# More dense filler products in a recurrent-attention and gated-MLP kernel, a longer warm-up, and two last stores on another queue

## The chip, the cores and the metric

The kernel runs on one core of a Trainium2 chip. The metric is the device time of one execution in microseconds (us), from the launch to the last store. TensorE (PE in the rows) multiplies matrices into PSUM, VectorE (DVE), ScalarE (ACT) and GpSimd (POOL) work element by element, and SyncE (SP) issues nearly all transfers. Each engine runs its instructions in program order. TensorE's clock has two levels here, 1.2 and 2.4 GHz; the rows give it as the granted clock, 0.50 or 1.00.

## What is computed

All inputs are float32. Three stages follow each other:

```python
for t in range(S):                                    # B, H, S, D = 4, 8, 768, 48
    cur = einsum('bhd,bhe->bhde', u * k[t], v[t])
    y[t] = einsum('bhd,bhde->bhe', r[t], state + cur)
    state = w * state + einsum('bhd,bhe->bhde', k[t], v[t])
x = y as [B * S, 384]
x = ((x @ w_a) * (x @ w_b)) @ w_out                   # 384 -> 1536 -> 384
out = (((x @ w1) * (x @ w2)) @ w3) @ w_out2           # 384 -> 1024 -> 1024 -> 384
```

## The kernel before

**The recurrence in chunks.** The 768 steps are cut into six chunks of 128 tokens (a chunk is called a step below, 0 to 5), each for four batches: 24 units, unit u being batch u % 4 of step u // 4. A unit computes scores r k with decay tables already multiplied in (`scores_h`, lines 365 and 369), the diagonal term with `u` (`scores_d`, line 377, whose moving operand has two columns), masks them on VectorE (`h_mask`, line 389), puts the diagonal in (`h_diag`, line 392), copies the rest on ScalarE (lines 397 and 400), and multiplies by the values: `y_0` (lines 499 and 504) for the units of step 0, which have no state yet, `y_mm` (lines 479 and 484) for step 1, with the state. The result is split into a high and a low part (lines 511, 514 and 517 in step 0; 537, 541 and 546 in step 1), because each large product is done as three: high by high, high by low and low by high.

**The large products.** `ab_mm` (line 639) multiplies the outputs by `w_a` and `w_b`, `m_mm` (lines 656 to 658) by `w_out`; both are mixed with the units of later steps. The weights arrive as 64-bit floats (`raw`, issued at lines 942 and 944) and are turned into float32 by three VectorE operations (lines 974, 978 and 982) and split into high and low (ScalarE line 987, VectorE line 990). The second pair of layers follows the same pattern with a table of sums (line 1293) and ends with `o` (lines 1396 to 1398), four evictions (lines 1417 and 1419) and the stores (line 1424).

**Filler products.** `busy(ps, n)` at line 284 multiplies the identity matrix by n copies of itself and writes 128 * n columns that nothing reads. It is called at three places: for the warm-up at the start (line 293, the table `WARM` of line 40), and at the end of `scores_d` for the units of step 0 (line 380), in the upper columns of the same PSUM bank as the diagonal, so that `h_diag` waits for it as well. A product of plain float32 operands is two records in the trace.

**The order.** `plan` (line 97) is a list scheduler: tasks with an engine, a cost estimate, dependencies, buffers and a priority are placed greedily, and each engine's program order is the order in which they were placed. The numbers given to `task` (0.9 at line 814, 0.4 at line 877, 5.8 at line 788) are such estimates; other numbers can give another order everywhere behind them.

Of the kernel before, what the change touches and what calls it, by code (L numbers as in the profile page):

```python
# [18 lines left out]
B, H, S, D = 4, 8, 768, 48  # L19
NP = H // 2  # L20
C = 128
# [3 lines left out]
KD = DM // 128  # L25
# [11 lines left out]
N64 = 61  # L37
SQ_LO, SQ_HI = 2e-9, 1e10

WARM = (4, 4, 4, 2)  # L40

SPLIT = 6
PAD = 288
# [125 lines left out]
def rwkv_moe_kernel(ctx, tc, rkT, nat, wu, wab, wout, w12, w3T, wo2, r_in, k_in, v_in, w_in, u_in, out):  # L169
# [13 lines left out]
    with tc.manual_schedule():  # L183
# [11 lines left out]
        def at_tile(shape):  # L195
            return psp.tile(shape, F32, tag=at_next[0], name=at_next.pop(0)[:-1])
# [87 lines left out]
        def busy(ps, n):  # L284

            mm(ps.rearrange("p (n c) -> p n c", n=n), lhsT=ident,
               rhs=ident.rearrange("p (o c) -> p o c", o=1).to_broadcast([128, n, 128]), start=True, stop=True)
# [83 lines left out]
        def scores_d(u):  # L371

            ps = at_tile([128, 512])
            at_ps["d", u] = ps[:, 0:H]
            e = alt[u % B][0:112, 2]
            for p in range(NP):
                mm(at_ps["d", u].rearrange("p (x n) -> p x n", x=2)[:, :, p], lhsT=e[:, p * C:(p + 1) * C], rhs=u_x[:, p],
                   start=(p == 0), stop=True, skip_group_check=True)
            if u < B:
                busy(ps[:, 256:512], 2)  # L380

        def bc4(t):
            return t.rearrange("p (o n) -> p o n", o=1).to_broadcast([128, 4, HALF])
# [104 lines left out]
        def y_0(u):  # L488

            vz = vz_t[u % 2]  # L490
            ps = at_ps["y", u] = at_tile([128, KD, C])
            a = a_t.pop(u)

            for n, e in enumerate((HALF, 128)):
                cs = slice(n * HALF, (n + 1) * HALF)
                for k in range(KD):
                    for x in range(2):
                        c = out_at(2 * k + x)
                        mm(ps[c:c + 64, k, cs], lhsT=vz[0:e, k, x, :], rhs=a[0:e, n, 4 * x + 3, :],  # L499
                           start=(k == 0 and n == 0), stop=False, skip_group_check=True)  # L500
                    for x in range(2):
                        h = 2 * k + x
                        c = out_at(h)
                        mm(ps[c:c + D, k, cs], lhsT=v_0[0:e, u, h * D:(h + 1) * D], rhs=a[0:e, n, 4 * x + k, :],
                           start=False, stop=True, skip_group_check=True)
# [164 lines left out]
        def task(*a, **k):  # L670
            t = Task(*a, **k)
            for b in t.bufs:
                b.users.append(t)
            tasks.append(t)
            return t

        def use(t, *bufs):
            for b in bufs:
                b.users.append(t)
            return t  # L680
# [93 lines left out]
        def due(us):  # L774
            return -3000.0 + 10 * us
# [9 lines left out]
            return [use(task("ACT", 0.6, lambda u=u: h_low(u), [ev], pu), ba)] + of  # L785

        tab = task("DVE", 5.2, lambda: None, [], due(-9))
        task("PE", 5.8, lambda: None, [], due(-9))
        task("ACT", 2.4, lambda: None, [], due(-9))
        task("POOL", 1.8, lambda: None, [], due(-9))  # L790
        m_one = [Slot(f"m{k}") for k in range(KD)]
# [9 lines left out]
        for u in range(B):  # L801
            pu = due(5 + 4 * u)
            rk_b[u] = fixed(W[("w1h", "w1l", "w2h", "w2l")[u]])
            W[("w4h", "w4l", "w5h", "w5l")[u]].users = alt_b[u].users
            lr = task("SP", 0.45, lambda u=u: load_rk(u), [], due(u), [rk_b[u]], size=0.45)
            lv = load_v[u] = task("SP", 0.45, lambda u=u: load_nat(u), [], due(u), [v_b] if u == 0 else [], size=0.19)
            use(lv, v_b)
            pz = use(task("ACT", 0.25, lambda u=u: prep_0(u, 3), [lv] + y_last.get(u - 2, []), pu), vz_b[u % 2], v_b)
            pu_ = use(task("POOL", 1.3, lambda u=u: prep_0(u, 2), [lr], pu), rk_b[u], alt_b[u])
            pk = use(task("DVE", 0.7, lambda u=u: prep_0(u, 0), [lr, tab], pu, sbuf=True), rk_b[u], alt_b[u])  # L810
            pr = use(task("DVE", 0.7, lambda u=u: prep_0(u, 1), [lr, tab, pk], pu, sbuf=True), rk_b[u], alt_b[u])
            bt, bd = [Buf(banks + at_s, none) for _ in range(2)], Buf(m_one, none)
            sc = use(task("PE", 1.2, lambda u=u, bt=bt: picked(bt, lambda: scores_h(u)), [pk, pr], pu, bt), alt_b[u])
            sd = use(task("PE", 0.9, lambda u=u, bd=bd: picked([bd], lambda: scores_d(u)), [sc, pu_], pu, [bd]), alt_b[u])
            m_old.append(sd)
            ba = Buf(a0_s, none)
            ev = halves(u, pu, sc, sd, bt, bd, ba)
            m_old += ev
            by = Buf(at_s, none)
            y = use(task("PE", 2.2, lambda u=u, by=by: picked([by], lambda: y_0(u)), ev + [pz], pu + 1, [by]),  # L820
                    ba, v_b, vz_b[u % 2])
            y_last[u] = [y]
            yh = use(task("ACT", 0.5, lambda u=u: y_0_evac(u), [y], pu + 2, [x_b[0]] if u == 0 else []), by, x_b[0])
            yr = use(task("PE", 0.2, lambda u=u: y_0_rest(u), [yh], pu + 2), by, x_b[0])
            xl_0.append(use(task("ACT", 0.5, lambda u=u: y_0_low(u), [yr], pu + 2), by, x_b[0]))
# [27 lines left out]
        for u in range(B, NU):  # L853
# [16 lines left out]
            if c == 1:  # L870
                bt, bd = [Buf(at_c, none) for _ in range(2)], Buf(at_c, none)
                al = alt_b[b]
                pu_ = use(task("POOL", 1.3, lambda u=u: prep_0(u, 2), [lr], pu - 9), rk_b[u], al)
                pk = use(task("DVE", 0.7, lambda u=u: prep_0(u, 0), [lr], pu - 9, sbuf=True), rk_b[u], al)
                pr = use(task("DVE", 0.7, lambda u=u: prep_0(u, 1), [lr, pk], pu - 9, sbuf=True), rk_b[u], al)
                sc = use(task("PE", 1.2, lambda u=u, bt=bt: picked(bt, lambda: scores_h(u)), [pk, pr] + after, pu, bt), al)
                sd = use(task("PE", 0.4, lambda u=u, bd=bd: picked([bd], lambda: scores_d(u)), [sc, pu_], pu, [bd]), al)
                ev = halves(u, pu - 60, sc, sd, bt, bd, ba)
                by = [Buf(at_c, none)]
                y = use(task("PE", 2.3, lambda u=u, by=by: picked(by, lambda: y_mm(u)), ev + s_up.get(u - B, []), pu + 1, by),  # L880
                        al, nat_b[u], ba)
                bs = [Buf(at_c, none)]
                sm = use(task("PE", 0.6, lambda u=u, bs=bs: picked(bs, lambda: s_mm(u)), kn + [y], pu + 2, bs), bk, nat_b[u])
                after = [y, sm]
                s_old, s_new = y, sm
            else:
                al = rk_b[u]
                t = use(task("POOL", 1.32, lambda u=u: prep_r(u, nc.gpsimd), [lr], pu - 9), rk_b[u])
                t = use(task("POOL", 1.32, lambda u=u: prep_k(u, nc.gpsimd), [t], pu - 9), rk_b[u])
                bp = Buf(pr_s, none)  # L890
                dg_b[u] = Buf(dg_s, none)
                d = use(task("POOL", 1.15, lambda u=u: prep_d(u, 0), [ln, load_u], pu - 8, [bp]), nat_b[u])
                d = use(task("POOL", 1.15, lambda u=u: prep_d(u, 1), [d], pu - 8), nat_b[u], bp)
                dg = use(task("DVE", 0.56, lambda u=u: prep_d(u, 2), [d], pu - 8, [dg_b[u]]), bp)
                by, bt = [Buf(at_s, none) for _ in range(2)], [Buf(banks, none) for _ in range(2)]
                sc = use(task("PE", 1.5, lambda u=u, bs=by + bt: picked(bs, lambda: state_scores(u)),
                              [t] + after + s_up.get(u - B, []), pu, by + bt), rk_b[u])
                of, ev = [], []
                for x in range(2):
                    ev = [use(task("DVE", 0.42, lambda u=u, x=x: a_mask(u, x), [sc] + ev, pu - 300, [] if x else [ba]), bt[x], ba)]  # L900
                    of.append(use(task("ACT", 0.28, lambda u=u, x=x: a_off(u, x), ev, pu - 300), bt[x], ba))
                ev = use(task("DVE", 0.77, lambda u=u: a_diag(u), ev + [dg], pu, sbuf=True), ba, dg_b[u])
                y = use(task("PE", 1.4 if kn else 1.1, lambda u=u: y_split(u), [ev] + of + kn, pu + 1), al, nat_b[u], ba, *by)
                if kn:
                    use(y, bk)
                after, bs = [y], by
                s_old, s_new = sc, y
# [344 lines left out]
        for pair in range(NB // 2):  # L1252
# [125 lines left out]
            for n in range(2):  # L1378
# [30 lines left out]
                for b in range(B):  # L1409
# [13 lines left out]
                    def st_out(e, be=be, r0=(2 * n + bt) * S + (2 * pair + c) * C):  # L1423
                        e.dma_start(out=out[r0:r0 + C, :], in_=be.ap[:, 0:DM])

                    q = "ACT" if end and b == B - 1 else "SP"
                    use(task(q, 0.1, lambda f=st_out, e=nc.scalar if q == "ACT" else nc.sync: f(e), [e], base + 800, size=0.2), be)


# [273 lines left out]
```

## Time and profile before

| what | value |
|---|---|
| runs of the kernel before | 865.78, 866.31 and 872.46 us; median 866.31 us |
| the profiled execution, its own time | 871.8 us |
| its span, from the first to the last instruction | 870.1 us |
| mean granted TensorE clock over the span | 0.978 |

All times inside the trace count from the start of the span of the profiled execution. A granted clock of 0.50 in a stretch means 1.2 GHz there.

### The profile page before, as it was taken

How to read it: one execution, taken by the hardware profiler on the slowest of the kernel's cores; microseconds unless marked ns; L12 is line 12 of the kernel's file. 1: busy time of each engine (PE TensorE's matmuls, PEld its weight loads, DVE VectorE, ACT ScalarE, POOL GpSimd, SP SyncE). 2: the span in 40 equal slices, each digit the busy share in tenths (PEclk: the TensorE clock that was granted, in tenths of full speed). 3: DMA queues.
4: the chain of work that ended last, by engine and by line, in shares of the span. 5: the costliest groups of instructions: out<-in, count | busy, mean ns of one | idle time of the engine just before them, and what ended most of it. 6: DMA issues, size and time to landing. Idle time of an engine off the chain costs nothing.

```text
span 870.1 us, 15683 instructions
## 1 busy us (share of the span) xinstructions
PE 853.7 (98%) x5959; PEld 718.6 (83%) x5959; DVE 571.3 (66%) x1038; ACT 402.7 (46%) x961; POOL 197.1 (23%) x162
## 2 busy tenths in 40 slices
PE   9989999999999999999999999999999999999996
PEld 6878888887788887787788888888888988898896
DVE  7598877367678878653476457626658845864652
ACT  5464343455565565333266656644327232623222
POOL 4112100223535204220100302212324501511120
PEclk7599999999999999999999999999999999999998
DMA  8554743456987977632254435346435344425202
GB/s 254 157 178 126 212 122 108 131 174 197 226 238 201 297 228 225 182 120 67 47 173 148 158 119 181 123 161 213 157 124 189 106 130 146 154 67 157 90 1 76
DMA packets 71409, 134.07 MB, mean 154 GB/s; under 512 B 8032, under 2 KB 47712, under 8 KB 71328
## 3 DMA queue, kind: packets, MB, share of 16 engines
q1 hardware_dynamic: 71184, 132.81, 50.1%
q8 instruction: 49, 0.80, 0.4%
q14 instruction: 32, 0.26, 0.1%
q10 hardware_dynamic: 144, 0.20, 0.1%
HBM read 107.94 MB, written 23.07 MB: 151 GB/s over the span
## 4 chain that ended last, share of the span: by engine, by line
PE 90%; DVE 4%; DMA 2%; SPq 1%; ACT 1%; issue 1%; DVEq 0%; ACTq 0%
PE ab L639 32%; PE ab L1293 14%; PE m L656 5%; PE m L657 5%; PE m L658 5%; PE at L1293 5%; PE at L1200 4%; PE o L1398 4%; PE o L1397 4%; PE o L1396 4%; PE at L456 1%; SPq L235 1%; PE at L414 1%; DMA wa<-w_d 1%; PE at L499 1%; DMA raw<-in_wab_dram 1%
## 5 line engine op out<-in xcount | busy, mean ns | idle before, releaser
L744 DVE TENSOR_TENSOR ab<-g,ab 128x512 f32<-128x512 f32 x72 | 50.0, 695 | 85.0 <-PE ab L639 60.3
L1366 DVE TENSOR_TENSOR qx<-qx,ab 128x512 f32<-128x512 f32 x95 | 64.0, 686 | 36.0 <-PE ab L1293 35.5
L656 PE MATMUL m<-gh,woh 128*128 128x512 f32 x216 | 85.0, 394 | 0.0
L657 PE MATMUL m<-gl,woh 128*128 128x512 f32 x216 | 84.2, 390 | 0.0
L658 PE MATMUL m<-gh,wol 128*128 128x512 f32 x216 | 84.2, 390 | 0.0
L743 ACT COPY g<-ab 128x512 f32<-128x512 f32 x72 | 42.1, 586 | 75.2 <-PE ab L639 71.8
L746 ACT CAST gh<-ab 128x512 fp32r<-128x512 f32 x72 | 42.3, 587 | 74.5 <-DVE ab L744 73.7
L1304 POOL TENSOR_TENSOR qx<-qx,qx 128x512 f32<-128x512 f32 x29 | 39.0, 1355 | 125.0 <-DVE qx L1366 117.1
L1386 ACT CAST gh<-qx 128x512 fp32r<-128x512 f32 x48 | 29.6, 620 | 75.2 <-PE o L1397 47.6
L749 DVE TENSOR_TENSOR gl<-ab,gh 128x512 fp32r<-128x512 f32 x72 | 49.4, 686 | 15.6 <-ACT gh L746 14.9
L1360 ACT ACTIVATE qx<-ab 128x512 f32<-128x512 f32 x56 | 33.0, 599 | 56.2 <-PE ab L1293 54.8
L1388 DVE TENSOR_TENSOR gl<-qx,gh 128x512 fp32r<-128x512 f32 x48 | 38.2, 802 | 31.0 <-ACT gh L1386 29.6
L978 DVE SCALAR_TENSOR_TENSOR cvt<-raw,cvt 128x512 int32<-128x512 int32 x61 | 48.7, 799 | 1.4
L639 PE MATMUL ab<-xt,wab0h 128*128 128x512 f32 x144 | 46.1, 401 | 2.3 <-ACT a_sc L440 2.3
L639 PE MATMUL ab<-xt,wab1h 128*128 128x512 f32 x144 | 46.9, 408 | 1.1 <-ACT a_sc L397 1.1
L656 PEld LDWEIGHTS m<-gh,woh 128*128 128x128 f32 x216 | 40.5, 188 | 8.7
L982 DVE SCALAR_TENSOR_TENSOR cvt<-raw,cvt 128x512 int32<-128x512 int32 x61 | 46.7, 765 | 1.5
L333 POOL TENSOR_TENSOR rk<-rk,tr 112x512 f32<-112x512 f32 x16 | 21.9, 1367 | 113.6 <-DMA rk<-in_rkT_dram 113.6
L658 PEld LDWEIGHTS m<-gh,wol 128*128 128x128 f32 x216 | 40.5, 188 | 8.5
L657 PEld LDWEIGHTS m<-gl,woh 128*128 128x128 f32 x216 | 40.6, 188 | 8.1
L639 PE MATMUL ab<-xt,wab3h 128*128 128x512 f32 x144 | 45.0, 393 | 2.0 <-ACT a_sc L440 2.0
L639 PE MATMUL ab<-xt,wab5h 128*128 128x512 f32 x144 | 44.6, 391 | 0.6 <-DVE gl L749 0.6
(334 smaller groups left out, 2282.6 us busy)
## 6 DMA issues: line engine op xcount, KB each, us to landing
tg<-t_d SPq DMA_DIRECT2D x45, 640.0 KB, 3.9
raw<-in_wab_dram SPq DMA_DIRECT2D x30, 512.0 KB, 4.6
rk<-in_rkT_dram SPq DMA_DIRECT2D x24, 448.0 KB, 5.5
t_d<-part SPq DMA_DIRECT2D x75, 128.0 KB, 3.0
raw<-in_wout_dram SPq DMA_DIRECT2D x18, 512.0 KB, 4.4
natt<-in_nat_dram SPq DMA_DIRECT2D x96, 96.0 KB, 4.0
raw<-in_w3T_dram SPq DMA_DIRECT2D x16, 512.0 KB, 3.6
raw<-in_w_dram SPq DMA_DIRECT2D x12, 512.0 KB, 4.0
```

The costliest lines, as they stand in the source:

```text
L639: mm(ps, lhsT=w[i][:, k, cs], rhs=x[:, j, k, :], start=(k + i + j == 0), stop=(k == KD - 1 and i == 1))
L656: mm(m_ps[q][k], lhsT=wh[:, j, cs], rhs=gh, start=first, stop=False)
L657: mm(m_ps[q][k], lhsT=wh[:, j, cs], rhs=gl, start=False, stop=False)
L658: mm(m_ps[q][k], lhsT=wl[:, j, cs], rhs=gh, start=False, stop=last)
L743: ea = use(task("ACT", D_A, lambda x=bg, y=ba: nc.scalar.copy(out=x.ap, in_=y.ap), [a], p0 + 1, [bg]), ba)
L744: mu = use(task("DVE", D_TT, lambda x=bg, y=bb: nc.vector.tensor_tensor(out=y.ap, in0=x.ap, in1=y.ap, op=ALU.mult), [ea, b], p0 + 2), bg, bb)
L746: hi = use(task("ACT", D_A, lambda x=bh, y=bb: nc.scalar.copy(out=x.ap[0], in_=y.ap), [mu], p0 + 2, [bh]), bb)
L749: nc.vector.tensor_tensor(out=x.ap[1], in0=y.ap, in1=x.ap[0], op=ALU.subtract)
L978: nc.vector.scalar_tensor_tensor(out=t["f"], in0=t["w"][:, :, 1], scalar=-0x40000000, in1=t["f"], op0=ALU.bitwise_and, op1=ALU.bitwise_or)
L982: nc.vector.scalar_tensor_tensor(out=t["f"], in0=t["w"][:, :, 0], scalar=29, in1=t["f"], op0=ALU.logical_shift_right, op1=ALU.bitwise_or)
L1293: mm(bank, lhsT=x, rhs=y, start=(start and n == 0), stop=(stop and n == 2), skip_group_check=True)
L1366: e = use(task("DVE", D_TT, lambda bv=bv, b=bank[c], s=s: nc.vector.tensor_tensor(out=bv.ap, in0=bv.ap, in1=b.ap, op=ALU.add if s > 0 else ...
```

## The change

It touches five places. The warm-up has five products of 512 columns where it had three of 512 and one of 256. `scores_d` ends with a filler of 384 columns in step 0 (256 before) and with one of 256 columns in step 1 (none before). `y_0` takes a fourth column block in its bank and begins with a filler of 128 columns. The scheduler's estimates for these tasks follow. Of the last four stores, the last two are issued by ScalarE (one before). In the changed kernel the lines from 493 on stand two lower.

```diff
-WARM = (4, 4, 4, 2)
+WARM = (4, 4, 4, 4, 4)
...
         def scores_d(u):
...
-            if u < B:
-                busy(ps[:, 256:512], 2)
+            n = 3 if u < B else 2
+            busy(ps[:, 128:128 + 128 * n], n)
...
         def y_0(u):
...
-            ps = at_ps["y", u] = at_tile([128, KD, C])
+            bank = at_tile([128, KD + 1, C])
+            ps = at_ps["y", u] = bank[:, 0:KD]
+            busy(bank[:, KD], 1)
...
-        task("PE", 5.8, lambda: None, [], due(-9))
+        task("PE", 6.6, lambda: None, [], due(-9))
...
-            sd = use(task("PE", 0.9, lambda u=u, bd=bd: picked([bd], lambda: scores_d(u)), [sc, pu_], pu, [bd]), alt_b[u])
+            sd = use(task("PE", 1.05, lambda u=u, bd=bd: picked([bd], lambda: scores_d(u)), [sc, pu_], pu, [bd]), alt_b[u])
...
-                sd = use(task("PE", 0.4, lambda u=u, bd=bd: picked([bd], lambda: scores_d(u)), [sc, pu_], pu, [bd]), al)
+                sd = use(task("PE", 0.85, lambda u=u, bd=bd: picked([bd], lambda: scores_d(u)), [sc, pu_], pu, [bd]), al)
...
-                    q = "ACT" if end and b == B - 1 else "SP"
+                    q = "ACT" if end and b >= B - 2 else "SP"
```

Three places show what this does to the order. The first is TensorE in step 1, from the end of unit 4's scores; `at` and `ab` are PSUM banks, `alt` the scaled r and k, `a_sc` the masked scores. Before:

```order
L377 MATMUL ab<-u_x,alt 128x2 x4
L567 MATMUL m<-v_99,k_98 48x48 x16
L639 MATMUL ab_579<-xt,wab0h 128x512 x2
L639 MATMUL ab_579<-xt,wab0l 128x512
L639 MATMUL ab_579<-xt,wab0h 128x512 x2
L639 MATMUL ab_579<-xt,wab0l 128x512
L479 MATMUL at<-alt,s_152 112x128 x4
L484 MATMUL at<-a_sc,natt 48x64 x16
L567 MATMUL at<-natt,kn 48x48 x8
L365 MATMUL ab<-alt 64x2x64 x2
```

Now:

```order
L377 MATMUL ab<-u_x,alt 128x2 x4
L286 MATMUL ab<-ident 128x256
L569 MATMUL m<-v_99,k_98 48x48 x16
L641 MATMUL ab_584<-xt,wab0h 128x512 x2
L641 MATMUL ab_584<-xt,wab0l 128x512
L641 MATMUL ab_584<-xt,wab0h 128x512 x2
L641 MATMUL ab_584<-xt,wab0l 128x512
L479 MATMUL at<-alt,s_153 112x128 x4
L484 MATMUL at<-a_sc,natt 48x64 x16
L569 MATMUL at<-natt,kn 48x48 x8
L641 MATMUL ab_584<-xt,wab0h 128x512 x2
L641 MATMUL ab_584<-xt,wab0l 128x512
```

The filler of 256 columns stands behind the two-column products, and unit 5's scores, which came right after line 567 before, now stand behind six groups of three `ab_mm` products.

The second is VectorE at units 2 and 3 of step 0 (`a_377` and `a_413` before, `a_380` and `a_415` now, are their masked scores). Before:

```order
L389 TENSOR_TENSOR a_377<-ab,mask_h 128x256 x2
L392 COPY_PREDICATED a_377<-ident_h,m 128x512
L990 TENSOR_TENSOR wab0l<-cvt,wab0h 128x512
L389 TENSOR_TENSOR a_413<-ab,mask_h 128x256
L389 TENSOR_TENSOR a_413<-at,mask_h 128x256
L392 COPY_PREDICATED a_413<-ident_h,m 128x512
L597 TENSOR_TENSOR alt<-rk,tr 112x512
```

Now:

```order
L389 TENSOR_TENSOR a_380<-ab,mask_h 128x256 x2
L599 TENSOR_TENSOR alt<-rk,tr 112x512
L392 COPY_PREDICATED a_380<-ident_h,m 128x512
L389 TENSOR_TENSOR a_415<-ab,mask_h 128x256
L389 TENSOR_TENSOR a_415<-at,mask_h 128x256
L392 COPY_PREDICATED a_415<-ident_h,m 128x512
L992 TENSOR_TENSOR wab0l<-cvt,wab0h 128x512
```

The scaling of unit 4's k (line 597, now 599) comes before unit 2's diagonal, and the low part of the first converted weights comes behind unit 3's diagonal.

The third is the end of ScalarE's program, where `o` is a finished PSUM bank and `qx` its copy. Before and now, as one piece:

```order
-L1419 COPY qx_7082<-o 128x384 x2
-L1419 COPY qx_6606<-o 128x384
-L1419 COPY qx_6475<-o 128x384
-L1419 COPY qx_6606<-o 128x384
-L1424 DMA out_dram<-qx_6606 128x384
+L1421 COPY qx_7091<-o 128x384 x2
+L1421 COPY qx_6615<-o 128x384
+L1421 COPY qx_6484<-o 128x384
+L1426 DMA out_dram<-qx_6484 128x384
+L1421 COPY qx_6615<-o 128x384
+L1426 DMA out_dram<-qx_6615 128x384
```

The last store but one is issued by ScalarE between its last two evictions.

## Rows read from the trace of the kernel before

**Rows 1.** The page: busy time by engine (share of the span, instructions).

```profile
PE 853.7 (98%) x5959; PEld 718.6 (83%) x5959; DVE 571.3 (66%) x1038; ACT 402.7 (46%) x961; POOL 197.1 (23%) x162
```

**Rows 2.** Stretches of the span: busy us and instructions by engine, granted clock, DMA.

```profile
core 0: us, PE busy (x) PEld busy (x) DVE busy (x) ACT busy (x) POOL busy (x), PEclk, DMA share, GB/s
...
12.00:12.50 0.50, 0.50 (x4) 0.50 (x5) 0.50 (x3) 0.01 (x1) 0.10 (x1) 0.61 1.10 303
...
13.00:39.00 26.00, 26.00 (x320) 21.53 (x323) 15.87 (x30) 10.06 (x26) 5.21 (x4) 0.50 0.60 182
39.00:39.50 0.50, 0.50 (x20) 0.50 (x22) 0.21 (x1) 0.49 (x3) 0.00 (x0) 0.58 1.08 320
...
63.50:64.00 0.50, 0.50 (x2) 0.40 (x2) 0.40 (x2) 0.32 (x1) 0.00 (x0) 0.50 1.17 402
64.00:66.50 2.50, 2.50 (x7) 1.92 (x7) 2.47 (x5) 1.25 (x3) 0.00 (x0) 0.50 0.97 374
66.50:67.00 0.50, 0.50 (x4) 0.37 (x3) 0.50 (x2) 0.00 (x0) 0.00 (x0) 0.78 0.27 107
```

**Rows 3.** Longer stretches behind, same columns.

```profile
42.00:92.00 50.00, 47.47 (x480) 38.66 (x474) 45.70 (x84) 26.70 (x70) 11.96 (x9) 0.97 0.53 158
...
130.00:864.00 734.00, 728.17 (x4831) 617.12 (x4829) 466.39 (x850) 341.60 (x812) 171.97 (x133) 1.00 0.49 151
```

**Rows 4.** TensorE in order of time: start us, us, line, operation [idle before, releaser].

```profile
1.48 5.15 PE L286 MATMUL m<-ident 128*128 128x512 f32 x8 [1.48 <-POOL ident L272]
...
8.91 1.05 PE L377 MATMUL m<-u_x,alt 112*128 112x2 f32 x8
9.82 0.68 PE L286 MATMUL m<-ident 128*128 128x256 f32 x2
10.83 0.32 PE L365 MATMUL ab<-alt 48*64 48x128 f32 x1 [0.33 <-DVE alt L600]
...
38.85 0.48 PE L365 MATMUL ab<-alt 48*64 48x128 f32 x2
...
63.23 1.17 PE L639 MATMUL ab<-xt,wab1h 128*128 128x512 f32 x2 [1.09 <-ACT a_sc L397]
```

**Rows 5.** The chain that ended last, start us and us, two pieces.

```profile
29.88 1.06 PE m L286 x2
...
72.42 0.68 PE ab L639 x3
```

**Rows 6.** VectorE's waits from 12 to 42 us: us in total, times, longest.

```profile
DVE a L392 <- PE m L286: 4.4, 2, 2.3
DVE a L389 <- PE ab L369: 2.7, 1, 2.7
DVE wab0l L990 <- ACT wab0h L987: 2.5, 1, 2.5
DVE a L389 <- PE at L369: 0.6, 1, 0.6
DVE a_sc L392 <- PE ab L377: 0.4, 1, 0.4
DVE a_sc L389 <- PE ab L369: 0.3, 1, 0.3
```

**Rows 7.** TensorE's waits from 130 us to the end.

```profile
PE ab L639 <- ACT a_sc L440: 4.4, 3, 2.0
PE ab L639 <- DVE gl L749: 0.6, 1, 0.6
PE ab L1293 <- DVE qx L1366: 0.2, 1, 0.2
```

**Rows 8.** All engines at the end, in order of time (q: a queue's issue).

```profile
863.01 1.42 SPq L1424 DMA_DIRECT2D out_dram<-qx  x1
...
863.54 0.48 ACT L1419 COPY qx<-o 128x384 f32<-128x384 f32 x1 [0.56 <-PE o L1398]
864.05 0.37 ACTq L1424 DMA_DIRECT2D out_dram<-qx  x1
```

## The prediction

> **What bounds the kernel now.** I read the busy shares first: TensorE is busy 98% of the span, VectorE 66%, the others less [rows 1]. Behind 130 us TensorE waits only 5.2 us in 734 (4.4 + 0.6 + 0.2) [rows 3, 7], so whatever an early stage gains or loses on TensorE is carried to the end almost unchanged. The granted clock by stretches comes next, since a busy engine need not be a quick one: from about 12.1 us (0.61 is the mean of a half microsecond that ends at 0.50) to about 39.4, 27.3 us, TensorE is busy without a gap at half the clock, 1.2 GHz, and once more from 63.5 or a little earlier to about 66.7 us [rows 2]. Ahead of the first fall it ran two-column products, 0.68 us of filler and an idle 0.33 us; ahead of the second it was idle for 1.09 us [rows 4]. Third, I ask what else could bound the 27.3 us. VectorE waits there for TensorE, or for ScalarE behind TensorE, 10.9 us in all (4.4 + 2.7 + 2.5 + 0.6 + 0.4 + 0.3) [rows 6]: TensorE sets the pace of the stretch. The four times shown are two pairs, 865.78 and 866.31 against 872.46 and the profiled 871.8. The traced one has the long stretch at half clock; what the shorter ones had no row shows. This is the largest unknown here.
>
> **The change part by part.** I sum against the profiled execution's own 871.8 us (span 870.1), which lies 5.5 us above the median of 866.31.
>
> *The clock in step 0.* If the added columns keep the clock at 1.00, the 27.3 us of TensorE work shrink by at most half, 13.6 us. VectorE keeps its order and its own work, so the stretch can't lose more than the 10.9 us that it waits. Each of these seven waits leaves a hand-over; the two smallest took 0.3 and 0.4 us [rows 6]. Seven times 0.3 is 2.1, which leaves 8.8; I take 9.0. The ends: 10.9, and 5.8, the distance between the two pairs of times, if that is what a full clock gives. VectorE is busy 45.7 of 50 us from 42 to 92 and TensorE 47.5 [rows 3]; both move forward together with their loads, so I let the gain survive.
>
> *The clock at 63.5 us.* 3.2 us at half clock are worth 1.6 at most. VectorE is full there (2.47 of 2.50) [rows 2]; I take 1.0, the ends being 0 and 1.6.
>
> *The warm-up.* Six more blocks of 128 columns (20 against 14). A block costs 5.15 / 14 = 0.37 us by the warm-up's row [rows 4], and by the filler at half clock, 1.06 us on the chain for two blocks [rows 5], 0.53 at half and 0.265 at full clock. Six are 1.6 to 2.2 us. They end later than the tables need them, so they push unit 0's scores; before unit 1's, TensorE now waits 0.33 us for VectorE [rows 4], and that is the only cover. I take 1.6 - 0.3 = 1.3, the upper end 1.9.
>
> *Step 0's columns.* Four units, two more blocks each: 8 x 0.265 = 2.1 us at full clock, 8 x 0.53 = 4.2 at half. At full clock the halved TensorE work (13.6 less) would run ahead of what VectorE allows (10.9 less) by 2.7 us, which covers up to all of the 2.1; but the block in `scores_d` stands ahead of the diagonal, which waits for it (4.4 us for two such waits) [rows 6]. I take 1.0, between 0 and 2.1. Without that cover, at half clock, it is the whole 4.2.
>
> *Step 1's columns.* Four units, two blocks each: again 2.1 us. TensorE has `ab_mm` products queued there, so little hides it; one block pair falls into the 1.09 us idle at 62.1 us [rows 4] if that place stays, worth 0.5. I take 1.6, ends 1.6 and 2.1.
>
> *The store.* SP's issue of the last store but one takes 1.42 us, until 864.43; ScalarE's issue takes 0.37 and the evictions leave it 0.56 us of room [rows 8], so it would be out at about 863.4 and delay nothing. The last store, out at 864.42, ends at the same moment, so the end hardly moves: -0.3, ends -1.0 and 0.
>
> *The order.* The diagonal of unit 2 now has the scaling of unit 4 ahead of it, and unit 5's scores stand behind six groups of `ab_mm`, 6 x 0.68 = 4.1 us [rows 5]. The same work is done in both orders; I take 0 and keep the 4.1 us, less the 0.7 that was ahead of them in any case, as a rival.
>
> Sum: 871.8 - 9.0 - 1.0 + 1.3 + 1.0 + 1.6 - 0.3 = **865.4 us**. With the good ends it is 871.8 - 10.9 - 1.6 + 1.3 + 0 + 1.6 - 1.0 = 861.2; with the bad ones 871.8 - 5.8 - 0 + 1.9 + 2.1 + 2.1 = 872.1. Against the median the forecast is 0.9 us less, 0.1%: no difference that can be measured (about 1% is what a measurement tells from no change).
>
> **The rivals.**
> *First: the shorter runs already had the full clock.* Then there is nothing to gain on the median, and the added work is all that is left: 866.0 + 1.3 + 1.0 + 1.6 - 0.3 = 869.6. For it speaks that 5.8 us between the pairs is a plausible part of the 10.9; against it that the stretch ought to be worth more.
>
> *Second: the clock falls as before.* Ahead of the fall stand the same two-column products, with 128 columns more behind them; then every added block costs double in step 0: 871.8 + 1.3 + 4.2 + 2.1 - 0.3 = 879.1, slower than the median by 1.5%. If the runs are like the shorter pair it is 866.0 + 7.3 = 873.3. It decides if the granted clock from 13 to 39 us stays below about 0.7: there the halved share of 9.0 no longer pays the 7.3. The row that speaks for it is the stretch itself: TensorE was busy 26.00 of 26.00 us, filler included, and the clock stayed at 0.50 [rows 2]; being busy was not enough. The Trainium skill, "TensorE: Matmul & The Clock Gate", Part 1, "What's actually happening", says that the throttled clock is the default and that activity releases it. Taken by busy time this case's trace does not agree: 26 us of it released nothing, and adding more activity to an engine already 100% busy would then change nothing, which is this rival's 879.1; taken as dense columns it would be the forecast.
>
> *Third: the new order makes a wait.* If unit 5's scores are late for VectorE by the 3.4 us they moved, the time is 865.4 + 3.4 = 868.8. Against it: VectorE has conversions between them.
>
> *Fourth: all good ends,* 861.2.
>
> **How the numbers follow.** The forecast 0.45, the first rival 0.20, the second 0.15 (two thirds of it at the longer time), the third 0.10, the good ends 0.10. No case reaches 857.6, so faster by over 1% gets 0.04 for what I have not seen; slower by over 1%, above 875.0, is the longer time of the second rival and a little, 0.11; the rest, 0.85, is within 1%. The range is 861.0 to 874.0; outside lie 0.10 of the second rival and some 0.06 at the lower edge.
>
> **What would show it.** Right: the granted clock is 1.00 through most of 13 to 39 us, the waits of the diagonal for the filler fall from 4.4 us to about 1, the scores of unit 4 begin near 30 us where TensorE had them at 38.85 [rows 4], and 63 to 67 us has no fall. Wrong: a clock of 0.50 over a like stretch (second rival); a clock of 1.00 with times as before or above (first); a new wait of some 3 us at unit 5's mask (third); a last store that lands a microsecond earlier or later would only correct the small term.

## The result and the profile after

The changed kernel takes 860.24 us (median of eight runs, 859.06 to 861.19), and the kernel before, in the eight runs beside it, 870.58 us (864.92 to 874.31). The ratio is 0.989, interval 0.986 to 0.992. The forecast was 865.4 us, so the kernel is 5.2 us quicker than I said, and 0.8 us quicker than the lower edge of the range, 861.0.

More than the median changed. The runs of the kernel before spread over 9.4 us, those of the changed one over 2.1. One hundred further runs of the kernel before, taken beside the experiments, say why: they go from 855.27 to 874.88 us (median 864.15), their mean granted clock from 0.974 to 0.998, and the two go together (correlation -0.85). A straight line through the hundred is 857.9 us at a clock of 1.000 plus 6.0 us for each 0.010 that is missing; single runs scatter about it by 2.4 us (standard deviation). One sentence on the ratios: runs over 1.5% above the shortest of their kernel are left out of them, and here a clock that falls makes such runs by itself, so beside each ratio I give the median and the clock of all runs.

The profiled execution takes 860.08 us of its own time, span 858.4, mean granted clock 0.998, against 871.8, 870.1 and 0.978 before. Its busy shares:

```profile
PE 845.4 (98%) x5977; PEld 710.5 (83%) x5977; DVE 573.3 (67%) x1038; ACT 401.2 (47%) x961; POOL 199.1 (23%) x162
```

TensorE has 18 records more than in [rows 1] (the added products) and is busy 8.3 us less; the share is 98% in both. The share could not have shown the gain. The stretches could, and they are where to look first:

```profile
core 0: us, PE busy (x) PEld busy (x) DVE busy (x) ACT busy (x) POOL busy (x), PEclk, DMA share, GB/s
12.00:39.50 27.50, 26.40 (x501) 21.70 (x501) 24.63 (x42) 16.12 (x47) 6.27 (x5) 1.00 0.76 230
39.50:56.00 16.50, 13.89 (x166) 10.94 (x165) 16.05 (x32) 9.29 (x25) 2.97 (x2) 1.00 0.62 189
56.00:60.00 4.00, 4.00 (x15) 3.34 (x15) 3.06 (x6) 1.20 (x2) 0.00 (x0) 0.57 0.62 227
60.00:100.00 40.00, 40.00 (x297) 32.95 (x296) 35.66 (x63) 17.18 (x38) 7.99 (x6) 1.00 0.62 170
```

The granted clock is 1.00 over the whole of what ran at 0.50 in [rows 2]; in 27.5 us TensorE ends 501 matmuls, where it ended 320 in 26. One fall is left, from about 56.5 to 60 us. TensorE in order of time:

```profile
1.48 6.44 PE L286 MATMUL m<-ident 128*128 128x512 f32 x10 [1.48 <-POOL ident L272]
...
10.13 1.05 PE L377 MATMUL m<-u_x,alt 112*128 112x2 f32 x8
11.05 0.89 PE L286 MATMUL m<-ident 128*128 128x384 f32 x2
11.87 0.32 PE L365 MATMUL ab<-alt 48*64 48x128 f32 x1
...
14.53 0.38 PE L286 MATMUL at<-ident 128*128 128x128 f32 x2
...
30.05 0.33 PE L365 MATMUL ab<-alt 48*64 48x128 f32 x2
...
34.79 0.74 PE L641 MATMUL ab<-xt,wab0h 128*128 128x512 f32 x2 [1.10 <-ACT a_sc L397]
...
55.69 1.11 PE L377 MATMUL ab<-u_x,alt 112*128 112x2 f32 x8 [1.48 <-DVE s L589]
56.66 1.20 PE L286 MATMUL ab<-ident 128*128 128x256 f32 x2
```

The warm-up is 1.29 us longer than in [rows 4] (6.44 against 5.15). Unit 1's scores start at 11.87 instead of 10.83 us, without the idle 0.33; unit 4's at 30.05 instead of 38.85, 8.8 us sooner. At 55.69 TensorE has waited 1.48 us for VectorE; the filler behind it is still 1.20 us long where the same 256 columns took 0.68 at full clock: it is the first row of the fall.

From there I follow the lead along the program, before against after. Unit 4's scores: 8.8 us. The first `ab_mm` (42.20, now 34.79): 7.4. The tables of the second stage (106.43, now 100.25): 6.2. The first product of the third stage (493.24, now 482.24): 11.0. The last issue of a store (864.05, now 854.09): 10.0. The end of the span: 11.7. So the change had 8.8 us, lost 2.6 up to the tables, won another 4.8 between 106 and 493 us, where it adds nothing, lost 1.0, and found 1.7 behind the last store. Of the 2.6 us, 1.2 are idle time: between unit 4's scores and the tables TensorE was idle for 2.5 us before and is for 3.7 now; the other 1.4 are longer busy time, with step 1's columns in it. TensorE's waits behind 130 us show part of the 4.8:

```profile
PE ab L641 <- ACT a_sc L440: 0.8, 1, 0.8
PE o L1398 <- DVE qx L1306: 0.8, 1, 0.8
PE ab L423 <- ACT g L745: 0.5, 1, 0.5
PE at L456 <- issue: 0.2, 1, 0.2
PE ab L1295 <- DVE qx L1368: 0.2, 1, 0.2
```

The wait for the masked scores was 4.4 us in three pieces [rows 7] and is 0.8 in one. The wait of 0.8 us at line 1398 is new, and is most of the 1.0 us lost in the third stage; it stands in every trace with the new order and in none with the old one. The rest of the 4.8 is a fall of the clock in the kernel before that I had not seen; its stretches, and its TensorE in order of time:

```profile
107.00:230.00 123.00, 122.40 (x1044) 99.85 (x1043) 81.46 (x149) 60.28 (x150) 26.49 (x22) 1.00 0.53 152
230.00:250.00 20.00, 18.52 (x217) 14.96 (x217) 14.47 (x31) 11.72 (x35) 10.58 (x9) 0.91 0.91 261
```

```profile
236.35 0.73 PE L639 MATMUL ab<-xt,wab0h 128*128 128x512 f32 x2 [1.48 <-ACT a_sc L440]
...
239.26 1.22 PE L639 MATMUL ab<-xt,wab0h 128*128 128x512 f32 x2
```

The same two products take 0.73 us after an idle of 1.48 us, and 1.22 three us later. 20 us at 0.91 lose up to 1.8 us of TensorE's work. In [rows 3] this is hidden: 1.8 in 734 us still reads 1.00. From the tables to the third stage TensorE is idle for 5.0 us before (386.81 us, 381.84 busy) and for 1.6 now (381.99 us, 380.36 busy): 3.3 of the 4.8 us are waits. The other 1.5 are shorter busy time, about what the fall cost.

VectorE's waits from 10 to 45 us, which were 10.9 us [rows 6], are these:

```profile
DVE cvt L976 <- DMA raw<-in_wab_dram: 1.3, 1, 1.3
DVE a L392 <- PE m L286: 1.2, 2, 0.8
```

### The profile page after: what moved, and what is told of

The parts are those of the page before. It is cut to its first block, busy times and chain, and to the rows that moved or that the text cites. A ratio compares the mean times of both kernels' runs of the same rounds, so it can differ in the third digit from the quotient of the medians.

```text
span 858.4 us, 15728 instructions
## 1 busy us (share of the span) xinstructions
PE 845.4 (98%) x5977; PEld 710.5 (83%) x5977; DVE 573.3 (67%) x1038; ACT 401.2 (47%) x961; POOL 199.1 (23%) x162
## 4 chain that ended last, share of the span: by engine, by line
PE 93%; DVE 2%; DMA 1%; ACT 1%; issue 1%; SPq 0%; POOL 0%; ACTq 0%; DVEq 0%; POOLq 0%
PE ab L641 33%; PE ab L1295 14%; PE m L658 6%; PE m L659 6%; PE m L660 5%; PE at L1295 5%; PE o L1398 4%; PE at L1202 4%; PE o L1400 4%; PE o L1399 4%; PE m L286 1%; PE at L456 1%; PE at L414 1%; PE ab L423 1%; DMA wa<-w_d 1%
## 5 line engine op out<-in xcount | busy, mean ns | idle before, releaser
L355 POOL TENSOR_TENSOR kn<-natt,tnat 128x384 f32<-128x384 f32 x12 | 14.0, 1168 | 133.7 <-PE at L467 121.9
L641 PE MATMUL ab<-xt,wab2h 128*128 128x512 f32 x144 | 45.0, 393 | 0.0
```

The costliest lines, as they stand in the source:

```text
L641: mm(ps, lhsT=w[i][:, k, cs], rhs=x[:, j, k, :], start=(k + i + j == 0), stop=(k == KD - 1 and i == 1))
```

## The experiments

Each kernel has ten runs. Diffs are against the changed kernel, unless said otherwise. My theory after the result: the added products work through the clock alone. Its rivals: the new order did it; or the store did.

Each run lists its mean granted clock. I call a run with less than 0.990 a fallen one; of the hundred runs of the kernel before 37 are. The sign is coarse: 0.010 of 858 us is about 17 us at half clock (an estimate), so shorter falls, as the one at 56 us in the changed kernel, don't show in it, and it doesn't say in which stage the clock fell. That is seen only in the one profiled run of each kernel.

### The order without the products, and the products without the order

`order_only` has the changed kernel's estimates and its order, and the filler products of before:

```diff
-WARM = (4, 4, 4, 4, 4)
+WARM = (4, 4, 4, 2)
...
-            n = 3 if u < B else 2
-            busy(ps[:, 128:128 + 128 * n], n)
+            if u < B:
+                busy(ps[:, 256:512], 2)
...
-            busy(bank[:, KD], 1)
```

> The order of the changed kernel (its scheduler estimates) with the filler products of the kernel before: warm-up of 14 blocks, 256 columns behind step 0's diagonal, none in step 1, none in y_0. If the products keep the clock, it falls to 0.50 near 12 us as in the trace before, for 10 us or more, and the time is 866 to 874. If the new order alone made the gain, the time is 858 to 862 whatever the clock does.

Measured: 867.19 us (857.69 to 872.95), before beside it 863.31; ratio 0.998 (0.992 to 1.003). Six of ten runs are fallen, five of them at 870.1 us or more with a clock of 0.973 to 0.979. The profiled run is one of these, 872.04 us, and its stretches show a fall like the one before, later and longer (from about 15.5 to 53.2 us):

```profile
12.00:14.00 2.00, 1.52 (x11) 1.12 (x10) 2.00 (x3) 0.50 (x2) 1.08 (x1) 1.00 1.07 382
14.00:53.00 39.00, 37.87 (x450) 32.19 (x451) 25.27 (x47) 17.38 (x49) 8.03 (x6) 0.52 0.53 152
53.00:55.00 2.00, 2.00 (x10) 1.68 (x9) 1.44 (x4) 0.92 (x3) 0.00 (x0) 0.94 0.98 286
```

TensorE is busy 37.87 of 39 us at 0.52. The order alone doesn't hold the clock, and its best run, 857.69, is no better than the best of before beside it, 857.95.

`products_only` has all of the added products and the estimates of before, so the order of before:

```diff
-        task("PE", 6.6, lambda: None, [], due(-9))
+        task("PE", 5.8, lambda: None, [], due(-9))
...
-            sd = use(task("PE", 1.05, lambda u=u, bd=bd: picked([bd], lambda: scores_d(u)), [sc, pu_], pu, [bd]), alt_b[u])
+            sd = use(task("PE", 0.9, lambda u=u, bd=bd: picked([bd], lambda: scores_d(u)), [sc, pu_], pu, [bd]), alt_b[u])
...
-                sd = use(task("PE", 0.85, lambda u=u, bd=bd: picked([bd], lambda: scores_d(u)), [sc, pu_], pu, [bd]), al)
+                sd = use(task("PE", 0.4, lambda u=u, bd=bd: picked([bd], lambda: scores_d(u)), [sc, pu_], pu, [bd]), al)
```

> The filler products of the change (and its store) with the scheduler estimates, and so the order, of the kernel before. If the products make all of the gain, the clock is 1.00 from 5 to 40 us and the time is 859 to 862, with unit 4's scores at about 30 us. If the part behind 107 us (4.8 us of the 11.7) comes from the order, unit 4's scores are at about 30 us all the same, the waits of ab_mm on ScalarE's a_sc behind 130 us are 3 to 4 us again, and the time is 863 to 866.

Measured: 861.04 us (859.27 to 869.56), ratio 1.0005 (0.997 to 1.004), no fallen run (0.992 to 0.998). Its longest run, at 0.992, is 6.8 us above the line, so not all of the spread is the clock. In its trace the clock is 1.00 to 44 us, unit 4's scores start at 30.63 us. The products hold the clock, whatever the order. TensorE's waits behind 130 us in it:

```profile
PE ab L641 <- ACT a_sc L440: 2.7, 3, 1.7
PE ab L641 <- DVE gl L751: 1.1, 3, 0.5
PE ab L1295 <- DVE qx L1368: 0.2, 1, 0.2
```

They are nearer to [rows 7] than to the changed kernel's. In the traces with the order of before `ab_mm` waits 2.7 to 4.4 us for `a_sc` there, in those with the new one 0.8 to 1.5, though with waits of up to 1.0 us more at line 456 (2.6 in `step0_none`). So the new order shortens these waits by one to three us in most traces, and gives 0.8 back at line 1398; whether it shortens the time by as much, the medians (861.04 against 860.24 to 860.59) don't resolve.

### The store

`store_only` is the kernel before with the moved store alone (this diff is against the kernel before):

```diff
-                    q = "ACT" if end and b == B - 1 else "SP"
+                    q = "ACT" if end and b >= B - 2 else "SP"
```

> The kernel before with only the store moved. A line through 62 runs of the kernel before gives 857.3 us at a mean clock of 1.000 and 6.3 us for each 0.010 below it. If the store is worth 1.6 us and nothing else of the change saves work, these runs lie 1.2 to 2 us below that line and scatter as widely in clock, 0.974 to 0.998. If the store is worth 0.3, they lie on the line.

`store_sp` is the changed kernel with that store back on SyncE's queue:

```diff
-                    q = "ACT" if end and b >= B - 2 else "SP"
+                    q = "ACT" if end and b == B - 1 else "SP"
```

> The changed kernel with its last store but one back on SP. From the start of ScalarE's last store to the end of the span the trace before has 6.05 us, the nine traces with the moved store 4.1 to 5.05. If the store makes this, the stretch is 5.8 to 6.3 us again and the time 861.5 to 863, above the changed kernel's 859.3 to 862.8. If it was the profile's own scatter, the stretch is 4.1 to 5.1 us and the time is unchanged within 0.3.

`store_only`: 867.63 us, before beside it 866.69, ratio 1.004 (1.000 to 1.008), seven of ten runs fallen; by the line through the hundred its runs are 0.9 us quicker than their clock would give (standard error 0.7), which fits neither 1.6 nor 0.3 better. `store_sp`: 860.25 us (858.46 to 861.42), ratio 0.996 (0.992 to 0.999), beside the changed kernel's medians of 860.24 and 860.59 (below) no change. The end of the changed kernel, and that of `store_sp`:

```profile
853.04 0.38 ACTq L1426 DMA_DIRECT2D out_dram<-qx  x1
...
853.58 0.48 ACT L1421 COPY qx<-o 128x384 f32<-128x384 f32 x1 [0.57 <-PE o L1400]
854.09 0.43 ACTq L1426 DMA_DIRECT2D out_dram<-qx  x1
```

```profile
853.50 0.33 SPq L1426 DMA_DIRECT2D out_dram<-qx  x1
...
854.03 0.48 ACT L1421 COPY qx<-o 128x384 f32<-128x384 f32 x1 [0.56 <-PE o L1400]
854.54 0.38 ACTq L1426 DMA_DIRECT2D out_dram<-qx  x1
```

SyncE's issue here takes 0.33 us, not the 1.42 of [rows 8]. From the start of the last issue to the end of the span it is 4.3 us with the moved store and 4.2 without (858.4 - 854.09, 858.7 - 854.54); in the kernel before it was 6.05, and in `store_only`, which moves it, 4.35. Only the one trace of the kernel before has the long end, so the 1.7 us are most likely scatter of that last transfer or of one issue; no effect of the store is shown.

### How many columns hold the clock in step 0

`step0_none` has no filler inside step 0, only the long warm-up and step 1's:

```diff
-            n = 3 if u < B else 2
-            busy(ps[:, 128:128 + 128 * n], n)
+            if u >= B:
+                busy(ps[:, 128:384], 2)
...
-            busy(bank[:, KD], 1)
```

> The changed kernel, same order and warm-up, with no filler at all inside step 0 (256 columns in step 1 kept). With 384 columns per unit no run of ten had a mean clock below 0.990, with 256 some had, up to six of ten. If the columns per unit decide how often the clock falls, all or nearly all runs are now below 0.985 and the median is 868 or more. If the order or the warm-up has a part in it, half of the runs or more stay at 0.990 and the median is below 863.

`step0_256` has 256 columns for 384 in step 0, and keeps all else:

```diff
-            n = 3 if u < B else 2
-            busy(ps[:, 128:128 + 128 * n], n)
+            busy(ps[:, 256:512], 2)
```

> The changed kernel, same order, with 256 columns behind step 0's diagonal as before (128 in y_0 kept, 256 in step 1 kept). If the 384 columns are needed, some runs fall to a mean clock of 0.985 or less (866 us or more). If the 128 columns in y_0 do it, the clock stays at 0.990 or above and the time is 0 to 1.1 us below the changed kernel.

`no_y0` leaves out the 128 columns in `y_0`:

```diff
-            busy(bank[:, KD], 1)
```

> The changed kernel, same order, without the 128 columns at the head of y_0. If these hold the clock in step 0, some runs show a mean clock of 0.985 or less and 866 us or more. If the 384 columns behind the diagonal hold it alone, all runs are at 0.990 or above and the best is 0.3 to 1.3 us below the changed kernel's best, as TensorE has waits at those places.

`short_warm` has the old warm-up:

```diff
-WARM = (4, 4, 4, 4, 4)
+WARM = (4, 4, 4, 2)
```

> The changed kernel with the old warm-up of 14 blocks. If the longer warm-up is what holds the clock, it falls near 12 us and the time is 866 to 872. If only the columns inside step 0 hold it, the clock stays at 1.00, unit 0's scores come 1.3 us earlier, unit 1's 0.3 to 1.3 us earlier, and the time is 858.8 to 860.2.

Measured, with all kernels put together by what stands inside step 0:

| columns behind the diagonal in step 0 | kernels | fallen runs | medians, us |
|---|---|---|---|
| none | step0_none | 8 of 10 | 865.31 |
| 256 | before; order_only; store_only | 37 of 100; 6 of 10; 7 of 10 | 864.15; 867.19; 867.63 |
| 256, with y_0's 128 and the long warm-up | step0_256 | 1 of 10 | 861.6 |
| 384 | products_only, short_warm, no_y0, no_step1, step1_384, store_sp, after_again, lean | 0 of 80 | 859.5 to 862.98 |

The ratios: `step0_none` 1.004 (1.000 to 1.009; before beside it 861.57), `step0_256` 0.999 (0.995 to 1.004), `no_y0` 0.9996 (0.996 to 1.003; median 860.98), `short_warm` 0.997 (0.995 to 0.9995; median 860.02). The stretch of `step0_none`:

```profile
12.00:30.00 18.00, 17.50 (x250) 15.65 (x252) 13.93 (x28) 8.52 (x23) 4.34 (x3) 0.58 0.67 208
30.00:34.00 4.00, 4.00 (x99) 3.57 (x97) 3.00 (x5) 2.27 (x7) 1.09 (x1) 0.75 0.97 244
```

TensorE is as busy as ever (17.50 of 18.00 us) and the clock falls. With 256 columns it falls in some executions and not in others (the profiled run of `store_only` is at 1.00 from 12 to 33 us), with 384 in none of those profiled. Of the eight kernels with 384, `no_y0` and `short_warm` each leave out one of the other two additions and have no fallen run, and `lean` below leaves out both. So 384 columns behind the diagonal are enough to hold step 0. That they are needed is not shown: `step0_256` keeps 256 there with `y_0`'s 128, the long warm-up and step 1's 256, and 1 of 10 fallen is not told from 0 of 10. Nor does it fit either of the two outcomes that were named for it; the columns can stand in `y_0` as well, as far as ten runs show.

`step0_none` fell less than its expectation had it: a median of 868 us or more and clocks below 0.985 were named, and it came to 865.31 at 0.984 to 0.987 in seven of its eight fallen runs. The fallen runs lie at 864.63 to 865.95 us (and one at 872.5) without filler, and in `order_only`, with 256, at 870.1 to 872.95 and 0.973 to 0.979 (and one at 864.28). The difference goes with the clock, so with a longer fall; what the columns themselves cost at half clock these runs don't separate.

`no_y0`'s best run, 857.28 us, is 1.8 us below the changed kernel's best, more than the 0.3 to 1.3 named; its profiled run, 857.44 us, is at a clock of 1.00 throughout.

### Step 1

`no_step1` leaves step 1's 256 columns out:

```diff
-            n = 3 if u < B else 2
-            busy(ps[:, 128:128 + 128 * n], n)
+            if u < B:
+                busy(ps[:, 128:512], 3)
```

> The changed kernel, same order, without step 1's filler. The sum had 1.6 to 2.1 us for this filler and 1.0 back for the clock. If the filler does nothing for the clock there (it falls at 56 us in the changed kernel too), the time is 1.5 to 2.1 us shorter, 858 to 858.7. If it holds a part of the clock, there are more or longer falls between 45 and 80 us and the time is 860 to 863.

`step1_384` makes them 384:

```diff
-            n = 3 if u < B else 2
-            busy(ps[:, 128:128 + 128 * n], n)
+            busy(ps[:, 128:512], 3)
```

> The changed kernel, same order, with 384 columns instead of 256 in step 1: 4 x 0.265 = 1.06 us more on TensorE at full clock. If the fall at 56 us is held off by denser filler, it is gone in most runs and pays 1.7, so the median is 859 to 860. If the idle time of TensorE at 46 and 55 us makes it, whatever the filler, it stays and the time is 860.5 to 862.

Measured: `no_step1` 862.98 us (ratio 0.999, 0.995 to 1.003), 2.4 us above the changed kernel taken again (below) by the medians of two chips; `step1_384` 861.47 us (ratio 0.998, 0.994 to 1.001). The stretches of `no_step1`:

```profile
12.00:46.00 34.00, 32.91 (x560) 26.73 (x559) 31.48 (x53) 18.89 (x54) 10.37 (x7) 1.00 0.79 236
46.00:58.00 12.00, 10.02 (x91) 7.74 (x92) 8.31 (x15) 5.72 (x14) 0.00 (x0) 0.57 0.23 79
58.00:60.00 2.00, 1.03 (x22) 0.60 (x14) 1.33 (x5) 0.93 (x4) 0.00 (x0) 1.00 1.05 395
60.00:66.00 6.00, 5.48 (x22) 4.67 (x23) 5.70 (x11) 2.07 (x5) 0.00 (x0) 0.72 0.39 148
```

Step 0 holds, and two falls come in step 1, where the changed kernel has one. One trace doesn't give this to the missing filler: that of `short_warm`, with the 256 columns, has two like them, the first of which reads:

```profile
46.00:56.00 10.00, 8.24 (x66) 6.72 (x65) 7.46 (x14) 3.93 (x9) 0.00 (x0) 0.57 0.12 48
```

The runs say more: five of ten of `no_step1` are at 0.992 or below, one of ten of `short_warm`, none of the eighteen of the changed kernel. With 384 columns the one fall is still there, and in the trace of `no_y0`, with 256, there is none:

```profile
56.00:60.00 4.00, 4.00 (x48) 3.42 (x48) 3.93 (x8) 1.83 (x3) 0.00 (x0) 1.00 0.14 56
```

So more columns at this place don't settle step 1. The row at 55.69 us above suggests why: the filler stands behind the two-column products in TensorE's program, and these wait 1.48 us for VectorE (line 589, which reads a PSUM bank), so the filler begins after the idle time and not in it. That the idle time makes the fall is not shown; a filler ahead of that wait, in a bank that is free, was not tried.

### The changed kernel again, and the smallest version

> The changed kernel once more, beside the kernel before on this chip. In 31 runs the kernel before took 857.95 to 873.35 (median 863.31), its mean clock falling from 0.997 to 0.977 as the time rises. If the change works by the clock alone, the changed kernel lies at 859 to 861.5 with every mean clock at 0.995 or above, 1 to 2 us above the best runs of the kernel before and 2 to 4 below its median. If it also saves work, its best run is below 857.9.

`after_again`, the changed kernel unaltered: 860.59 us (859.31 to 862.8; clock 0.995 to 0.999), before beside it 863.78; ratio 0.998 (0.996 to 1.001). The same kernel that was 1.2% below the median of its eight runs of before is 0.4% below that of another 31, since how many runs of before fall differs from sitting to sitting (medians 861.57, 863.31, 863.78, 866.69, 870.58).

`lean` keeps what the runs above speak for, 384 columns in step 0 and 256 in step 1, with the new order, and drops the long warm-up and the columns in `y_0`:

```diff
-WARM = (4, 4, 4, 4, 4)
+WARM = (4, 4, 4, 2)
...
-            busy(bank[:, KD], 1)
```

> The changed kernel, same order, with the old warm-up and without the 128 columns in y_0: of the change are left 384 columns behind step 0's diagonal, 256 in step 1, the order and the store. If the 384 columns alone hold the clock in step 0, no run has a mean clock below 0.990 and the median is 857.5 to 859.5, below the changed kernel and below the kernel before. If it takes all three, some runs fall to 0.985 or less (866 us or more) and the median is above 861.

Measured: 859.5 us (857.59 to 862.06), ratio 0.994 (0.991 to 0.998), no fallen run. Beside `store_sp`, which ran on the same chip, it is 0.75 us less, which the intervals (0.991 to 0.998 and 0.992 to 0.999) don't separate. Its clock is 1.00 from 5 to 40 us, and unit 4's scores start at 28.27 us. Two falls remain behind; on TensorE they begin so:

```profile
48.30 1.22 PE L640 MATMUL ab<-xt,wab0h 128*128 128x512 f32 x2 [1.50 <-ACT g L744]
...
57.52 1.38 PE L377 MATMUL ab<-u_x,alt 112*128 112x2 f32 x8 [1.48 <-DVE s L588]
58.76 1.20 PE L286 MATMUL ab<-ident 128*128 128x256 f32 x2
```

Both of its falls follow an idle TensorE of 1.5 us, as at 55.69 us in the changed kernel. By its median it is the quickest of all the kernels here, the two that are compared included.

## Why the prediction was right in its mechanism and 5 us too long

**The mechanism was right.** Three of the signs that I named came: a clock of 1.00 through 12 to 39 us, unit 4's scores near 30 us (30.05), the diagonal's wait for the filler down from 4.4 to 1.2 us. The fourth, no fall at 63 to 67 us, came by the letter alone, as the fall stands at 56.5 to 60 us instead. Up to the tables the sum agrees by luck. It gave 9.0 - 1.3 - 1.0 = 6.7 us up to unit 4 (measured 8.8) and 6.7 + 1.0 - 1.6 = 6.1 up to the tables (measured 6.2): two errors of 2 us cancel.

**The terms.** The clock's 9.0 was too little: from unit 1's scores to unit 4's the changed kernel is 9.8 us shorter (8.8 and a start 1.04 us later), step 0's columns already paid; with the 1.0 that I reckoned for these it would be 10.8, just under the upper end of 10.9. That bound rested on "VectorE keeps its order", though the change gives VectorE another order at units 2 and 3; its waits went from 10.9 to 2.5 us. The warm-up's six blocks took 1.29 us where I had 1.6; unit 1's scores came 1.04 us later, with 0.21 for the longer filler behind unit 0's diagonal in it, so the net term is about 0.8 (an estimate) and not 1.3. Of the columns the hundred runs give a check: on the line through them, `order_only` lies 1.6 us (standard error 0.4) under the time for its clock, and the changed kernel taken again 1.1 (0.4) over it. By this pair the products cost 2.7 us at equal clock; I had 1.3 + 1.0 + 1.6 = 3.9. The figure is loose: `products_only` against the line, with the order of before in both, gives 1.6 (0.7), and `no_y0` at a clock of 1.000 took 857.44 us, below the line. The 1.0 us for the second fall was not gained: the fall stayed, 7 us earlier. Step 1 gave 2.6 us back where I reckoned 0.6: that 1.0, and 1.2 us of longer waits for which I had no term. The store's -0.3 is not distinguishable from 0.

**The step that failed** is "Behind 130 us TensorE waits only 5.2 us in 734", "so whatever an early stage gains or loses on TensorE is carried to the end almost unchanged". From 106 to 493 us the changed kernel won 4.8 us more, by waits that the new order shortened (5.0 to 1.6 us in all) and a further fall of the clock, at 237 us, that the mean of 1.00 over 734 us hid. I took the order at 0 and looked for a loss alone (the third rival, 868.8 us); a possible gain was owed as well, and the 5.2 us of waits were its size. The tail's 1.7 us, for which I had 0.3, are most likely scatter.

**The base.** "The four times shown are two pairs" was wrong. There is a continuum from 855 to 875 us, for the most part by how long the clock falls. The first rival, that the shorter runs were at full clock already, is half right: 19 of the hundred have 0.995 or more, at a median of 858.6 us, and the changed kernel doesn't beat those. It takes the long runs away. The quickest execution of all, 855.27 us, is one of the kernel before. By this rival the time would have been 869.6 us, because I set the full clock at 866; by the line it is 857.9, and with the products' 1.6 to 2.7 us 859.5 to 860.6.

**The other rivals.** The second (the clock falls as before, 879.1 or 873.3) fell with the first profile, but its argument was sound: at 256 columns or none TensorE was 97 to 100% busy at or near half clock. The Trainium skill, "TensorE: Matmul & The Clock Gate", Part 1, "What's actually happening", lets activity release the clock; taken as busy time this case's traces don't agree (37.87 of 39 us busy at 0.52). The third did not show. VectorE does not wait at unit 5's mask (46.39 us), and TensorE's wait at line 377, 1.48 us at unit 6 now, has its like in the kernel before, at unit 5:

```profile
49.77 1.02 PE L377 MATMUL at<-u_x,alt 112*128 112x2 f32 x8 [1.33 <-DVE s L587]
```

What did come is the 1.2 us of idle time in all. The fourth, all good ends, 861.2, came nearest, though not by its terms: its 1.6 us at the second fall weren't had. The chance of 0.04 for faster by over 1% rested on a median of three runs; against the first eight of before the change is over that bound, against the hundred (860.24 / 864.15, 0.5%) it isn't.

## What to carry to other kernels

Read the granted clock of every run before you take a median for the base: where it scatters, a change that holds it narrows the spread, and its gain on the median depends on how many runs fell, which three times don't show. Look for falls in stretches of 10 or 20 us, since a mean over hundreds hides a fall worth 2 us. Give a filler where small products follow each other, as few columns as hold the clock in ten runs. Where it should fill a wait, its place would be ahead of the wait and not behind; that is a conclusion from the order of TensorE's program, and no run here tries it.

## What the runs showed that I had not expected

One program on one core gave 857.69 to 872.95 us in ten executions (`order_only`), with the clock from 0.996 down to 0.973. The Trainium skill, "TensorE: Matmul & The Clock Gate", Part 1, "What's actually happening", says that where the clock changes at the start differs from run to run of one kernel, and puts what the start costs at under 1% of a usual span. The first no trace here shows: the first product of the warm-up takes 2.07 or 2.08 us in every one. What these runs show is scatter from falls inside the kernel, and that is more, 2.3% between the ends of the hundred runs.

Half measures can be the dearest: in the profiled runs, without filler the fall in `step0_none` ended near 32 us, with 256 columns it lasted to 39.4 us before and to about 53.2 in `order_only`, though in `store_only`'s there was none in step 0. And most falls that I looked up behind step 0 follow an idle TensorE of 1.1 to 1.5 us (63.23 and 236.35 us before, 55.69 after, 48.30 and 57.52 in `lean`). That is no rule: behind the idle 1.10 us at 34.79 us the changed kernel's clock stayed at 1.00, so did that of the kernel before behind the 1.33 at 49.77, and that of `lean` behind 1.42:

```profile
39.31 0.50 PE L640 MATMUL ab<-xt,wab0l 128*128 128x512 f32 x1 [1.42 <-DVE wab0l L991]
```

What tells these apart, and why `short_warm` fell near 48 us where `no_y0` didn't, stays open.
